# Another order of all steps of a gated MLP behind linear attention, and the low part of one w_sg tile through TensorE

## The chip, the cores and the metric

One core of a Trainium2 chip runs the whole kernel. The metric is the device time of one execution in microseconds, the median of the runs that are shown. Engines are named as the profile names them: PE is TensorE, PEld its weight loads, DVE is VectorE, ACT is ScalarE, POOL is GpSimd, SP is SyncE, which here only issues transfers.

## What is computed

Eight batches of eight heads, 576 positions of 64 channels. A linear attention first (softmax of q over its channels, softmax of k over positions), then a gated MLP on the heads' output x (576 x 512 for each batch):

```python
q_s = softmax of q over the channels          # exp(q - max) / (sum + 1e-9)
k_s = softmax of k over the positions
kv = np.einsum('bhsd,bhse->bhde', k_s, v)
x = np.einsum('bhsd,bhde->bhse', q_s, kv)     # heads side by side: 576 x 512

h = gelu(x @ w_in)                            # 512 x 1024, tanh form
u, v = h[..., :512], h[..., 512:]
v_n = (v - mean) / sqrt(var + 1e-6) * g_ln    # over the 512 channels
v_s = np.einsum('ts,bsd->btd', w_sg, v_n) + b_sg
out = x + (u * v_s) @ w_out                   # 512 x 512
```

w_in and w_out come as 64-bit numbers, the rest in 32 bits.

## The kernel before

All matmuls of the MLP run in three passes of a reduced 32-bit format: each operand is split into a high part (`_h`, the value rounded by a cast) and a low part (`_l`, the rest), and high x high, low x high and high x low are added in PSUM. So most steps come in such pairs: `x_high` and `x_low`, `wi_h` and `wi_l`, `gate_high` and `gate_low`.

The kernel is a list of some 1,220 named steps, `PLAN` (lines 28 to 129), each with its batch and tile numbers and, where there is a choice, the engine (A for ACT, V for DVE, G for POOL). The loop at line 657 calls them in that order. `InOrder` (line 136) ties every instruction of SP, DVE, ACT and POOL to the one before it on the same engine, and `mm` (line 231) does that for TensorE; so the list alone sets the order on every engine, and an instruction that waits holds back all behind it on its engine. Data and buffers are tracked by the tile framework, which puts in the waits between engines.

The steps, in the order in which a batch b goes through them:

- `load_q`, `load_k`, `load_v` (each for half h of the heads) and the loads of the weights are transfers that SP issues. Two halves have two buffers, so `load_k 1 0` overwrites what `kv_mm 0 0` reads.
- `wi_a` to `wi_d` take the bits of a 128-column tile f of w_in from 64 to 32 bits (ACT, then three times DVE); `wi_h` and `wi_l` split it. `wi_l` has three ways: POOL, DVE (V), or ACT (A) from PSUM after `wi_x`, in which TensorE adds identity x value and (minus identity) x high part. `wo_a` to `wo_l` do the same for w_out, `ws_h` and `ws_l` for tile i of w_sg (five tiles; the fifth is the tail of 64 rows).
- `k_ma`, `k_mb`, `k_mc`, `kt_mm`, `k_top`, `kb_mm`, `k_sub`, `k_exp`: maximum of k over positions (DVE, two transposes on TensorE between), subtraction and exp. `q_max`, `q_swapm`, `q_top`, `q_sub`, `q_exp`, `q_sum`, `q_swapd`, `q_inv`, `q_mul`, `q_turn`: softmax of q and its transposition.
- `kv_mm`, `kv_inv`, `kv_scale`, `x_mm`: the two products of the attention. `x_high` and `x_low` split x; `x_low` runs on DVE, or on ACT after `x_neg`, in which TensorE subtracts the high part in PSUM.
- `hu_mm` and `hv_mm`: x @ w_in for u (four tiles) and v (four tiles, and a fifth, the tail, for two batches at once). `hv_gelu`, `hv_sq`, `hv_stat`, `hv_pow`, `hv_norm`, `hv_high`, `hv_low`: activation and normalisation of v; `tail_high`, `tail_low`, `tail_again` for the tail.
- `sg_mm` multiplies with w_sg; its last two matmul pairs take the tail (`vn_1`, `vn_2`) and the bias. `gate`, `gate_high`, `gate_low`: product with u. `out_mm`, `out_add`, `out_rest`, `out_store`: product with w_out, x added, store.

PSUM has three double tiles (`ps2`: x, u, gate and output products, and in turn) and two single ones (`ps1`: the rest). So TensorE can start such a product when the one three (or two) before it in the same set was read out.

In the names of the trace below, `ps` is any PSUM tile, `ot_i` a tile of w_in under conversion, `vnh`, `vnl` and `vn` are the parts of v_n and of its tail, `km` and `qm` maxima, `raw_...` the buffers of 64-bit weights.

Of the kernel before, what the change touches and what calls it, by code (L numbers as in the profile page):

```python
# [28 lines left out]
load_q 0 1, q_max 0 1, q_swapm 0 1, q_top 0 1, q_sub 0 1 V, load_eye, load_w_in 0, load_w_in 1, load_q 0 0, load_b, load_w_in 3, load_k 0 1  # L29
load_w_in 2, load_k 0 0, load_w_in 5, wi_a 0, load_w_sg 2, load_v 0 0, load_w_sg 1, load_w_in 6, wi_a 1, neg, load_g, load_w_in 7, load_w_sg 0, wi_b 0  # L30
load_w_in 4, q_exp 0 1, wi_b 1, wi_c 0, load_v 0 1, load_w_out 0, wi_c 1, q_max 0 0, wi_a 3, q_swapm 0 0, wi_d 1, wi_d 0, wi_b 3, q_top 0 0, k_ma 0 1
wi_c 3, q_sum 0 1, q_sub 0 0, wi_h 1, wi_d 3, b_h, wi_h 0, wi_a 2, q_swapd 0 1, k_ma 0 0, wi_h 3, wi_x 1, wi_x 0, wi_b 2, k_mb 0 0, k_mb 0 1
q_exp 0 0, wi_l 0 A, wi_c 2, k_mc 0 1, k_mc 0 0, q_inv 0 1, wi_d 2, wi_l 1 A, kt_mm 0 0, k_top 0 0, wi_h 2, wi_x 3, q_sum 0 0, ws_h 2, q_mul 0 1 0
b_l, kb_mm 0 0, wi_l 3 A, k_sub 0 0, q_swapd 0 0, k_exp 0 0, kt_mm 0 1, k_top 0 1, kb_mm 0 1, q_inv 0 0, ws_l 2 V, wi_a 5, wi_a 7, kv_mm 0 0
k_sub 0 1, q_mul 0 0 0, load_k 1 0, q_mul 0 0 1, k_exp 0 1, wi_x 2, q_turn 0 0, kv_inv 0 0, q_mul 0 1 1, q_turn 0 1, kv_scale 0 0, wi_a 4, wi_l 2 A
ws_h 0, wi_b 7, x_mm 0 0, wi_b 4, wi_c 7, kv_mm 0 1, wi_c 4, x_high 0 0, x_high 0 1, wi_d 7, ws_l 0, wi_h 7, x_neg 0 1, x_neg 0 0, load_k 1 1
kv_inv 0 1, q_turn 0 3, q_turn 0 2, kv_scale 0 1, wi_a 6, x_low 0 0 A, wi_x 7, x_low 0 1 A, load_q 1 1, wi_d 4, load_w_out 1, load_w_out 3, x_mm 0 1
load_q 1 0, wi_h 4, wi_b 5, k_ma 1 0, wi_b 6, wi_x 4, x_high 0 2, x_high 0 3, k_mb 1 0, k_ma 1 1, x_neg 0 3, wi_l 7 A, k_mc 1 0, x_neg 0 2, wi_c 5
k_mb 1 1, ws_h 1, kt_mm 1 0, wi_c 6, k_mc 1 1, q_max 1 1, k_top 1 0, ws_l 1, wi_l 4 A, x_low 0 3 A, x_low 0 2 A, hu_mm 0 0, wo_a 0, q_swapm 1 1
kt_mm 1 1, kb_mm 1 0, wi_d 6, hu_mm 0 2, q_top 1 1, wi_d 5, k_top 1 1, q_max 1 0, wo_a 3, wi_h 6, wi_h 5, q_sub 1 1, k_sub 1 0, kb_mm 1 1, q_swapm 1 0  # L40
hu_mm 0 1, wi_l 6, q_exp 1 1, q_top 1 0, wo_b 3, k_sub 1 1, q_sub 1 0, k_exp 1 0, q_sum 1 1, k_exp 1 1, wi_l 5 V, wo_b 0, wo_c 3, q_swapd 1 1
load_v 1 0, load_v 1 1, kv_mm 1 0, hv_mm 0 0, load_v 2 0, load_k 2 0, load_w_out 2, load_w_sg 4, q_exp 1 0, q_inv 1 1, kv_inv 1 0, kv_scale 1 0
hu_gelu 0 1, q_mul 1 1 0, q_sum 1 0, hv_mm 0 3, q_mul 1 1 1, q_turn 1 2, q_swapd 1 0, wo_d 3, hv_gelu 0 0, q_inv 1 0, wo_c 0, hv_mm 0 2, hu_gelu 0 2
wo_a 1, q_mul 1 0 0 V, hv_gelu 0 3 A, hu_gelu 0 0, wo_b 1, q_turn 1 3, q_turn 1 0, q_mul 1 0 1, wo_a 2, kv_mm 1 1, q_turn 1 1, hv_gelu 0 2 A
# [131 lines left out]
def gmlp_kernel(ctx: ExitStack, tc: tile.TileContext, q, k, v, w_in, g_ln, w_sg, b_sg, w_out, identity, out):
# [529 lines left out]
```

## Time and profile before

| | |
|---|---|
| runs of the kernel before | 523.53, 519.97, 523.24 us |
| median | 523.24 us |
| profiled execution | 520.9 us, its span 519.1 us |
| granted clock of TensorE, mean | 0.99 |
| busy: PE, DVE, ACT, POOL | 489.8, 353.8, 258.7, 125.7 us |

The span runs from the first to the last instruction of the profiled execution; the time of an execution has a little around it. Idle time of an engine that is not the bound costs nothing. Durations of instructions that follow each other closely overlap by some hundredths of a microsecond.

### The profile page before, as it was taken

To read this page: it belongs to the slowest core of one execution; us is meant where nothing else is said; L and a number is where in the kernel's file an instruction comes from. 1 tells how busy PE (TensorE), PEld (TensorE's weight loads), DVE (VectorE), ACT (ScalarE), POOL (GpSimd) and SP (SyncE) were. 2 spreads that over 40 slices of the span, in tenths; PEclk is the share of its full clock that TensorE was granted. 3 is DMA by queue.
4 is the path that set the end of the run, shared out by engine and by line. 5 is a ranking of instruction groups with operands and counts; after the bars stand their busy time and mean duration, and the time that the engine had idled before them with its cause. 6 is when DMAs were issued, how large, how long until landed. Compare 5 with 4: busy or idle time off the path is not lost.

```text
span 519.1 us, 9328 instructions
## 1 busy us (share of the span) xinstructions
PE 489.8 (94%) x3852; PEld 447.0 (86%) x3852; DVE 353.8 (68%) x595; ACT 258.7 (50%) x506; POOL 125.7 (24%) x103
## 2 busy tenths in 40 slices
...
GB/s 284 377 208 270 218 169 1 2 97 115 131 162 129 98 3 137 1 52 47 223 50 70 61 232 19 29 1 189 108 1 0 47 47 1 1 0 69 2 23 92
DMA packets 19054, 48.87 MB, mean 94 GB/s; under 512 B 1602, under 2 KB 8132, under 8 KB 19012
## 3 DMA queue, kind: packets, MB, share of 16 engines
...
q14 instruction: 12, 0.10, 0.1%
...
## 4 chain that ended last, share of the span: by engine, by line
PE 81%; DVE 12%; DMA 4%; issue 1%; SPq 0%; ACT 0%; DVEq 0%
PE ps L232 81%; DVE ot_i L146 2%; DMA qq<-q 2%; DVE km L146 2%; DMA raw_vnh<-w_in 2%; DVE qm L146 1%; DVE ot_o L146 1%; DVE qd L146 1%; DMA kk<-k 1%; DVE qt L146 1%; DVE vnl L146 1%; DVE x_l L146 1%; DVE v L146 1%; SPq L146 0%; DVE o L146 0%
## 5 line engine op out<-in xcount | busy, mean ns | idle before, releaser
L146 POOL TENSOR_TENSOR rs<-ve,half 128x1 f32<-128x1 f32 x36 | 26.8, 753 | 141.4 <-DVE ve L146 141.4
L232 PE MATMUL ps<-ws_h,vnh 128*128 128x288 f32 x256 | 56.1, 300 | 0.0
L232 PE MATMUL ps<-gh,wo_h 128*128 128x288 f32 x256 | 56.0, 297 | 0.0
L232 PE MATMUL ps<-ulow,wo_h 128*128 128x288 f32 x256 | 55.5, 295 | 0.0
L232 PE MATMUL ps<-gh,wo_l 128*128 128x288 f32 x256 | 55.3, 295 | 0.0
L232 PE MATMUL ps<-ws_l,vnh 128*128 128x288 f32 x256 | 54.9, 295 | 0.0
L232 PE MATMUL ps<-ws_h,vnl 128*128 128x288 f32 x256 | 54.8, 295 | 0.0
L146 DVE TENSOR_TENSOR u<-ps,u 128x576 f32<-128x576 f32 x32 | 23.9, 752 | 43.2 <-PE ps L232 41.3
L146 ACT CAST gh<-u 128x576 fp32r<-128x576 f32 x32 | 21.1, 670 | 54.2 <-DVE u L146 54.1
L146 DVE TENSOR_TENSOR o<-ps,x_h 128x576 f32<-128x576 f32 (+1 forms) x33 | 23.6, 731 | 28.5 <-PE ps L232 28.5
L232 PEld LDWEIGHTS ps<-ws_h,vnh 128*128 128x128 f32 x256 | 41.4, 189 | 1.1 <-DVE u L146 0.4
L232 PEld LDWEIGHTS ps<-gh,wo_h 128*128 128x128 f32 x256 | 41.3, 188 | 0.6
L232 PEld LDWEIGHTS ps<-ws_h,vnl 128*128 128x128 f32 x256 | 41.3, 188 | 0.0
L232 PEld LDWEIGHTS ps<-gh,wo_l 128*128 128x128 f32 x256 | 41.3, 188 | 0.0
L232 PEld LDWEIGHTS ps<-ws_l,vnh 128*128 128x128 f32 x256 | 41.3, 188 | 0.0
L232 PEld LDWEIGHTS ps<-ulow,wo_h 128*128 128x128 f32 x256 | 41.3, 188 | 0.0
L146 ACT ACTIVATE v<-ps 128x512 f32<-128x512 f32 x36 | 21.4, 597 | 39.2 <-PE ps L232 37.5
L146 POOL TENSOR_TENSOR ulow<-u,gh 128x576 fp32r<-128x576 f32 x12 | 17.4, 1453 | 96.2 <-ACT gh L146 96.0
L232 PE MATMUL ps<-x_h,wi_h 128*128 128x288 f32 x256 | 40.5, 300 | 0.0
L232 PE MATMUL ps<-wi_h,x_h 128*128 128x512 f32 x144 | 40.1, 400 | 0.0
L232 PE MATMUL ps<-wi_l,x_h 128*128 128x512 f32 x144 | 39.5, 395 | 0.0
L232 PE MATMUL ps<-wi_h,x_l 128*128 128x512 f32 x144 | 39.3, 395 | 0.0
(105 smaller groups left out, 1068.1 us busy)
## 6 DMA issues: line engine op xcount, KB each, us to landing
...
```

The lines of the kernel that those rows point to most:

```text
L146: ins = op(*args, **kw)
L232: tc.keep_in_program_order(nc.tensor.matmul(*args, **kw))
```

## The change

The table of steps is replaced as a whole by another order of nearly the same steps. What differs in kind:

- w_sg tile 0 gets its low part from ACT out of PSUM, after a new step `ws_x 0` of TensorE (as `wi_x` does for w_in); before, POOL made it.
- `x_neg` with `x_low` on ACT is kept for pairs 0 and 1 of batch 0 only; before, also for pairs 2 and 3 of batch 0 and pair 1 of batch 1. These `x_low` now run on DVE.
- `wi_x` is there for tiles 0, 3, 5 and 6 of w_in; before, for 0, 1, 2, 3, 4 and 7. Tiles 2 and 7 get their low part on DVE (before: 5), tiles 1 and 4 on POOL (before: 6).
- ws_l 1 goes from POOL to DVE, ws_l 4 from DVE to POOL. Many of `hv_gelu`/`hv_stat`, `gate_low`, `out_rest`, `q_mul` and `q_sub` change engine, in both directions.
- `b_l` may be given an engine (it is not), and functions for another way to the sum of q, with an input for it, are new but no step of the list calls them (`load_blk`, `qs_mm`, `q_rec`, `qr_mm`, `q_by`).

```diff
 PLAN = """
-load_q 0 1, q_max 0 1, q_swapm 0 1, q_top 0 1, q_sub 0 1 V, load_eye, load_w_in 0, load_w_in 1, load_q 0 0, load_b, load_w_in 3, load_k 0 1
+load_w_in 1, load_w_in 3, load_w_in 0, load_w_in 2, load_q 0 0, load_eye, load_k 0 0, load_q 0 1, load_w_in 6, wi_a 1, load_w_sg 2, load_w_sg 1
...
-    kr_s = slots("kr", 2, [P, 2])
+    kr_s, qr_s = slots("kr", 2, [P, 2]), slots("qr", 2, [QC, 4 * NQ])
+    blk = sb("blk", [P, 2])
...
+    def ws_x(i):
+
+        ps = bank(ps2, "sx", i)
+        for j in range(2):
+            cs = slice(j * (WT // 2), (j + 1) * (WT // 2))
+            mm(ps[:, j, 0:WT // 2], eye, raw_sg(i)[:, cs], start=True, stop=False)
+            mm(ps[:, j, 0:WT // 2], minus, (ws_h[:, i] if i < ST else ws_1)[:, cs], start=False, stop=True)
+
     def ws_l_(i, E=G):
         hi, lo = (ws_h[:, i], ws_l[:, i]) if i < ST else (ws_1[0:TL], ws_2[0:TL])
+        if E is A:
+            A.copy(out=lo.rearrange("p (j n) -> p j n", j=2), in_=st["sx", i][0:lo.shape[0], :, 0:WT // 2])
+            return
         E.tensor_tensor(out=lo, in0=raw_sg(i)[0:lo.shape[0]], in1=f32(hi), op=ALU.subtract)
...
+    arr["blocks"] = np.ascontiguousarray(np.repeat(np.eye(2, dtype=np.float32), D, axis=0))
```

The first place is SP's queue, some 20 transfers into the program. In the names, `kk0_0` and `kk1_0` are k of batches 0 and 1, half 0 (one buffer), `vv0_1` is v of batch 0, half 1, `ghws_...` a raw tile of w_sg, `raw_wo_...` raw tiles of w_in at this point, `raw_x_h` one of w_out. Before:

```order
L146 DMA ghws_0_132<-w_sg 128x640
L146 DMA raw_wo_h_88<-w_in 128x4x256
L146 DMA vv0_1_139<-v 128x1300
L146 DMA raw_x_h_89<-w_out 128x4x256
L146 DMA kk1_0_251<-k 128x1280
L146 DMA kk1_1_313<-k 128x1280
```

And in the changed kernel:

```order
L148 DMA raw_wo_h_88<-w_in 128x4x256
L148 DMA kk1_0_250<-k 128x1280
L148 DMA ghws_4_261<-w_sg 128x640
L148 DMA vv0_1_264<-v 128x1300
L148 DMA raw_x_h_90<-w_out 128x4x256
L148 DMA g_bc_67<-g_ln 128x512
```

The load of k for batch 1 stood behind both loads of v of batch 0, and now stands ahead of the second, with the fifth tile of w_sg between them.

The second place is DVE just ahead of the first `sg_mm`. `vnl` is the low part of v_n (`hv_low`), `vn_10` the tail (`tail_low 0`), the last thing that the first `sg_mm` needs; `qm2_0` and `qm2_1` are the row maxima of q of batch 2 (`q_top`), `km2_1` maxima of k. Before:

```order
L146 SCALAR_TENSOR_TENSOR vnl_788<-v0_1_747,rs0_1_811,vnh_787 128x512
L146 TENSOR_TENSOR km2_1_829<-km2_1_829 128x256
L146 SCALAR_TENSOR_TENSOR vnl_788<-v0_2_634,rs0_2_847,vnh_787 128x512
L146 TENSOR_TENSOR qm2_0_844<-qm2_0_844,qs2_0_871 128x36
L146 TENSOR_TENSOR km2_1_829<-km2_1_829,kk2_1_672 128x256
L146 SCALAR_TENSOR_TENSOR vn_10_71<-v0_4_832,rs0_4_880,vn_10_71 64x512
```

And in the changed kernel:

```order
L148 SCALAR_TENSOR_TENSOR v0_2_744<-v0_2_744,nm0_2_776,g_bc_67 128x512
L148 SCALAR_TENSOR_TENSOR vnl_756<-v0_0_638,rs0_0_742,vnh_755 128x512
L148 TENSOR_TENSOR qq2_0_641<-qq2_0_641,qm2_0_709 128x1152
L148 SCALAR_TENSOR_TENSOR vnl_756<-v0_2_744,rs0_2_819,vnh_755 128x512
L148 SCALAR_TENSOR_TENSOR vn_10_71<-v0_4_801,rs0_4_844,vn_10_71 64x512
L148 TENSOR_TENSOR km2_1_814<-km2_1_814,kk2_1_654 128x256
L148 TENSOR_REDUCE qm2_1_905<-qq2_1_688 128x36
```

The maxima of q of batch 2, half 1, and the last one of k have moved behind the tail.

The third place is POOL at the same point of the program, from the last `hv_pow` of batch 0 (`rs0_4`) on; `qq2_1<-qq2_1,qm2_1` is `q_sub 2 1`, `wo_l` the low part of w_out. Before:

```order
L146 TENSOR_TENSOR rs0_4_880<-ve0_4_865,half_70 128x1
L146 TENSOR_TENSOR rs1_2_928<-ve1_2_877,half_70 128x1
L146 TENSOR_TENSOR qq2_1_654<-qq2_1_654,qm2_1_809 128x1152
L146 TENSOR_TENSOR wo_l_695<-ot_o_2_610,wo_h_694 128x4x128
L146 TENSOR_TENSOR wo_l_695<-ot_o_0_403,wo_h_694 128x4x128
```

And in the changed kernel:

```order
L148 TENSOR_TENSOR rs0_4_844<-ve0_4_841,half_70 128x1
L148 TENSOR_TENSOR wo_l_600<-ot_o_1_452,wo_h_599 128x4x128
L148 TENSOR_TENSOR qq2_1_688<-qq2_1_688,qm2_1_905 128x1152
L148 TENSOR_TENSOR rs1_3_1006<-ve1_3_965,half_70 128x1
L148 TENSOR_TENSOR qq2_0_641<-qq2_0_641,qd2_0_953 128x576
L148 TENSOR_TENSOR wo_l_600<-ot_o_2_529,wo_h_599 128x4x128
```

One low part of w_out has moved ahead of `q_sub 2 1`, the other two behind it; and `q_sub 2 1` needs `qm2_1`, which DVE now makes behind the tail.

## Rows read from the trace of the kernel before

**Rows 1.** The page: span, and busy time of each engine.

```profile
span 519.1 us, 9328 instructions
PE 489.8 (94%) x3852; PEld 447.0 (86%) x3852; DVE 353.8 (68%) x595; ACT 258.7 (50%) x506; POOL 125.7 (24%) x103
```

**Rows 2.** The chain that ended last, in order of time: start, length, what.

```profile
135.73 378.25 PE ps L232 x2970
```

**Rows 3.** Timeline of TensorE: start, length, instructions, in brackets idle time before.

```profile
28.02 2.44 PE L232 MATMUL ps<-vv,kk 128*64 128x65 f32 x40 [0.28 <-ACT kk L146]
...
32.95 1.39 PE L232 MATMUL ps<-vv,kk 128*64 128x65 f32 x40
...
38.65 1.12 PE L232 MATMUL ps<-ot_i,eye 128*128 128x512 f32 x2
...
39.99 0.80 PE L232 MATMUL ps<-x_h,minus 128*128 128x288 f32 x4
...
40.92 1.31 PE L232 MATMUL ps<-x_h,wi_h 128*128 128x288 f32 x8
...
83.57 0.43 PE L232 MATMUL ps<-ws_h,vnh 128*128 128x288 f32 x2
...
86.50 0.42 PE L232 MATMUL ps<-ws_l,vnh 128*128 128x288 f32 x2
89.94 0.80 PE L232 MATMUL ps<-ws,vn 128*128 128x288 f32 x4 [3.02 <-DVE vn L146]
...
106.42 0.54 PE L232 MATMUL ps<-gh,wo_h 128*128 128x288 f32 x2
...
135.73 0.44 PE L232 MATMUL ps<-eye,km 128*128 128x128 f32 x2 [0.43 <-DVE km L146]
```

**Rows 4.** Windows: stretch, length, busy PE, PEld, DVE, ACT, POOL, clock, DMA, GB/s.

```profile
0.00:90.00 90.00, 66.22 (x487) 50.30 (x487) 82.25 (x144) 67.24 (x145) 37.17 (x29) 0.94 0.63 220
20.00:30.00 10.00, 6.57 (x47) 4.17 (x49) 9.18 (x17) 7.06 (x14) 5.41 (x5) 0.52 0.99 342
40.92:83.57 42.65, 42.53 (x317) 35.77 (x316) 41.36 (x77) 35.23 (x85) 19.31 (x14) 1.00 0.50 184
136.00:514.00 378.00, 377.97 (x2970) 353.11 (x2968) 226.19 (x378) 166.36 (x316) 76.33 (x65) 1.00 0.19 63
```

**Rows 5.** Timeline of DVE just ahead of the first sg_mm's wait.

```profile
82.82 0.19 DVE L146 TENSOR_TENSOR qm<-qm,qs 128x36 f32<-128x36 f32 x1
...
83.65 0.42 DVE L146 TENSOR_TENSOR km<-km 128x256 f32<-128x256 f32 x1
...
84.64 2.13 DVE L146 TENSOR_TENSOR qm<-qm,qs 128x36 f32<-128x36 f32 x1
86.69 1.53 DVE L146 TENSOR_TENSOR km<-km,kk 128x256 f32<-128x256 f32 x1
88.26 1.63 DVE L146 SCALAR_TENSOR_TENSOR vn<-v,rs,vn 64x512 fp32r<-64x512 f32 x1
```

**Rows 6.** Timeline of POOL in the same stretch.

```profile
84.11 2.61 POOL L146 TENSOR_TENSOR qq<-qq,qm 128x1152 f32<-128x1152 f32 x1
86.68 2.67 POOL L146 TENSOR_TENSOR wo_l<-ot_o,wo_h 128x512 fp32r<-128x512 f32 x2
```

**Rows 7.** Groups of DVE instructions: busy us, mean ns of one, idle before.

```profile
L146 DVE TENSOR_REDUCE qm<-qq 128x36 f32<-128x1152 f32 x16 | 21.5, 1348 | 16.5 <-DMA qq<-q 16.3
L146 DVE TENSOR_TENSOR x_l<-ps,x_h 128x576 fp32r<-128x576 f32 x27 | 19.9, 748 | 5.3 <-ACT x_h L146 5.2
...
L146 DVE TENSOR_TENSOR qq<-qq,qd 128x576 f32<-128x576 f32 x14 | 11.2, 819 | 0.0
...
L146 DVE SCALAR_TENSOR_TENSOR vn<-v,rs,vn 64x512 fp32r<-64x512 f32 x8 | 6.9, 858 | 3.3 <-ACT vn L146 3.2
```

**Rows 8.** Start of DVE; then, of the k tile from 25 to 60 us, issue to landing.

```profile
5.69 1.35 DVE L146 TENSOR_REDUCE qm<-qq 128x36 f32<-128x1152 f32 x1 [2.24 <-DMA qq<-q]
...
DMA to landing us min/median/max: 4.0/4.7/5.5
```

More of the change, by code (lines that the diff above doesn't have):

```diff
@@ L24 @@
 WT = S + TL
+NQ = 6
+QC = S // NQ
 PLAN = """
[L29 to L32 removed]
@@ L33 @@
[L33 to L44, printed above, removed]
@@ L61 @@
-x_high 2 0, q_swapd 3 0, load_v 3 1, hv_high 1 0, x_low 2 0, k_mc 3 0, hv_low 1 0, k_ma 3 1, kt_mm 3 0, kv_scale 2 1, hu_mm 1 0, q_inv 3 0, k_top 3 0
-q_swapm 3 1, x_high 2 1, q_top 3 1, x_low 2 1, k_mb 3 1, hu_gelu 1 2, hu_gelu 1 0, k_mc 3 1, q_sub 3 1 V, kt_mm 3 1, kb_mm 3 0, sg_mm 1 0, k_top 3 1
-q_exp 3 1, q_mul 3 0 1 V, k_sub 3 0, kb_mm 3 1, sg_mm 1 1, q_mul 3 0 0 V, q_sum 3 1, sg_mm 1 2, q_turn 3 1, k_sub 3 1, k_exp 3 1, gate 1 1, q_turn 3 0
-q_swapd 3 1, gate 1 0, load_q 4 0, k_exp 3 0, gate_high 1 1, gate_high 1 0, x_mm 2 1, gate 1 2, q_inv 3 1, kv_mm 3 0, x_high 2 3, gate_low 1 0
```

205 lines of the change are left out of this document (122 added, 83 removed).

## The prediction

> **What bounds the kernel now.** I read the page first: TensorE is busy for 489.8 of 519.1 us, VectorE (DVE) for 353.8 [rows 1]. That alone says that TensorE is the bound, but it is an average, so the next view is the chain that ended last: its last long piece is TensorE alone, 378.25 us and 2970 matmuls without a break, from 135.73 us on [rows 2]. The time by windows says the same of 136 to 514 us: 377.97 of 378 us busy, while DVE has 226.19 [rows 4]. No reordering can gain there; it can only lose. What is left to gain is ahead of 136 us. In the first 90 us TensorE is busy for 66.22 and DVE for 82.25 [rows 4]: DVE is the bound of the head. The timeline of TensorE shows what that costs: the first hu_mm 0 0 starts at 40.92, work is then dense up to 86.9, in the middle of the first sg_mm (started at 83.57), and there TensorE waits 3.02 us for DVE (tail_low 0, tile vn). One more wait of 0.43 us follows at 135.73 [rows 3].
>
> I therefore cut the time into three: up to the first hu_mm 0 0, from there to the first sg_mm, and from there to the end.
>
> **From the first sg_mm to the end.** Before: 519.1 - 83.57 = 435.5 us, of which 3.0 + 0.4 us are the two waits; 432.1 without them. The changed plan has the same steps of TensorE behind its first sg_mm, with kt_mm 2 0 moved in (two transposes, under 0.4 us), and the same five DVE additions and the same stores behind the last matmul. So 432.3 us, if TensorE never waits. Where a wait could come is the first out_mm 0: DVE has, by the mean durations of its steps, some 18 us of work between tail_low 0 and gate_low 0 3 (an estimate over 27 steps), and TensorE 16.5 us up to out_mm (89.94 to 106.42 [rows 3]), with some 2.4 us of slack, since out_mm takes the four gated tiles one after another; I cost it at nothing here and give the lack of that cover to a rival.
>
> **From hu_mm 0 0 to the first sg_mm.** 42.65 us before, 42.53 of it busy [rows 4]. The same steps after, less x_neg 1 1 (0.4 us: four such matmuls, two steps, took 0.80 [rows 3]) and two small pairs of transposes: 42.0 us.
>
> **Up to hu_mm 0 0.** Removed from TensorE: two of six wi_x (38.65 to 39.99, 1.34 us each) and two of four x_neg of batch 0 (0.4 us each); added: ws_x 0. No row shows ws_x; it is the same two kinds of matmul over 640 columns instead of 512, so 0 us (where TensorE sits idle anyway) to 640/512 x 1.34 = 1.7 us, twice that at the lower clock. It stands where TensorE waits for DVE, so I take nothing for it, nor for the removed ones as such. Functions and an input that the plan never calls cost nothing: they issue no instruction.
> What counts is when the data comes. DVE starts at 5.69 us when the first transfer (q) lands, and 576 KB of it [rows 8]; the first is now w_in 1, 512 KB, and one step of ScalarE on it, for which I allow 0.7 us: about 6.2 us. Ahead of k_sub 0 0 DVE then has about 5 us less to do than before (q_sub 0 1, both q_sum, q_inv 0 1 and the k maxima of half 1 come later, wi_l 2 comes in). But ScalarE now has ws_h 0, ws_h 2 and a swap ahead of k_exp 0 0, so that kv_mm 0 0, at 28.02 before, starts at about 25.2 and, at the 2.44 us that it took at half clock [rows 3], ends at 27.6. Here the order of SP's queue matters: load_k 1 0 overwrites kk 0 0 and so waits for kv_mm 0 0, and load_w_sg 4 and load_v 0 1 now stand behind it; before, both v loads stood ahead. A k load takes 4.7 us to land (4.0 to 5.5 [rows 8]): 32.4; the 970 KB behind it at 342 GB/s [rows 4] take 2.9 us more: v 0 1 is there at 35.2, with 4.0 or 5.5 in place of 4.7 at 34.5 or 36.0. Before, kv_mm 0 1 started at 32.95 and hu_mm 0 0 followed 7.97 us later [rows 3]; without x_neg 0 2 and 0 3 (0.8 us) 7.2 us. That gives 42.4 us, in bounds of 41.7 and 43.2. I take 42.3, so 1.4 us later than before, and the first sg_mm at 42.3 + 42.0 = 84.3.
>
> **Is DVE there in time?** The first sg_mm needs tail_low 0 3.35 us after its start: at 87.65. Before, DVE was through with it at 89.9, with 82.25 us of work and 7.65 idle [rows 4]. Two things change. First the list ahead of tail_low 0: out go q_max 2 1 (1.35), k_top 2 0, q_top 2 1 and k_mc 2 1 (together about 1.0), in come x_low 0 2, 0 3 and 1 1 (0.75 each), wi_l 7 and q_mul 0 0 1 (0.7 to 0.8 each): net +1.5 us [rows 7]. Second, the last three instructions before that wait took 2.13, 1.53 and 1.63 us, where the like of the first took 0.19 and of the second 0.42 just before, and the third takes 0.86 in the mean of its eight and 0.75 without this one [rows 5, 7]: together 3.9 us too long. Each ends when a POOL instruction ends: q_sub 2 1 ran from 84.11 for 2.61, then two wo_l from 86.68 for 2.67 [rows 6]. In the changed order q_sub 2 1 cannot start there, since q_top 2 1 and so its wait come behind tail_low 0, and wo_l 2 and wo_l 0 stand behind it on POOL; only wo_l 1 is left. So 82.25 + 1.5 - 3.9 = 79.9 of work, and, with the same idle time, DVE is through at 87.5. Bounds: 91.4 with none of the 3.9 gone, and as far below 87.5, 83.6, if as much again goes earlier in the head.
> The Trainium skill, SBUF — State Buffer, Who interferes with whom, states the rule behind these rows: a VectorE instruction with two inputs in SBUF and a GpSimd instruction that reads SBUF exclude each other, and the second waits out the first. The trace agrees in the three cases. By that rule the change also brings new chances of it, since it puts ws_l 1, wi_l 2, wi_l 7 and q_mul 0 0 1 on DVE, all with two SBUF inputs; by rows, it costs what rival 3 says.
>
> **The sum.** 84.3 + 432.3 = 516.6 us of span, against 519.1: -2.5. The profiled execution took 520.9, 1.8 more than its span, so 518.4 for the like of it. The median of the runs is 523.24, 2.3 over that execution; on it the same difference gives **520.7 us**.
>
> **Rivals.** (1) Ending slower: the SP queue. v 0 1 and w_sg 4 hang on kv_mm 0 0. ScalarE waits in order on ws_h 4 with b_h and x_high 0 0 behind it, TensorE on kv_mm 0 1. Each microsecond by which kv_mm 0 0 ends after 27.6 moves hu_mm 0 0, and the end, by one. Past 30.1 the gain is gone; at 33 the time is 526. For it speaks that every step ahead of kv_mm 0 0 is a chain of three engines; against it, that DVE has 5 us less ahead of it.
> (2) The clock. Between 20 and 30 us the granted clock was 0.52 on average, 1.2 for most of it instead of 2.4 GHz, in a stretch in which TensorE was busy for 6.57 of 10 us [rows 4]. After, TensorE has fewer steps before hu_mm 0 0 and new idle time while v 0 1 is on its way, so the lower level may last to 40 us: kv_mm 0 1 at 2.44 for 1.39 [rows 3], x_mm 0 1 and wi_x 5 about 1.2 more each: +3.5, so 524.2. The Trainium skill, TensorE: Matmul & The Clock Gate, Part 1, says that the lower level is the default and activity lifts it, which by itself gives the same 524.2.
> (3) DVE stays late: other pairs of DVE and POOL instructions collide as often (bound 91.4 above). The first sg_mm then waits 3.7 us as before: 524.4.
> (4) More than forecast: kv_mm 0 0 by 25, k and v landing at the short end, hu_mm 0 0 at 40, DVE ready at 84: -5 or better, 518 or less.
> (5) Nothing: what the head gains is lost in the first out_mm 0, where DVE's 18 us get 2 to 3 longer by collisions: 523.
>
> **Chances.** Forecast (518.5 to 522.5) 0.45; rival 1 0.14, rival 2 0.10, rival 3 0.10, rival 4 0.14, rival 5 0.07. About 1% is what a measurement of this kernel can tell from no change, since its own three runs lie 0.7% apart: faster by more is under 518.0, most of rival 4 and an edge of the forecast: 0.17. Slower by more is over 528.5, the far end of rivals 1 and 2, or an unseen wait in the dense part: 0.13. Within 1%: 0.70. The range from 515.5 to 526.5 holds the forecast, rivals 2, 3 and 5 and the near parts of 1 and 4.
>
> **What the changed profile would show.** hu_mm 0 0 at 42.3; the first sg_mm at 84.3 with no wait for vn in its last part over 0.5 us; no POOL instruction of 2 us beside tail_low 0; from the first out_mm 0 to the end TensorE without a wait over 0.5 us. Wrong would be a start of hu_mm 0 0 past 45 (rivals 1, 2: the clock row tells which), a wait for vn (rival 3), or waits behind 136 us, for which I saw no reason.

## The result, and the profile after

| | before | after |
|---|---|---|
| median (13 runs each) | 521.51 us (518.27 to 523.56) | 516.99 us (516.37 to 518.03) |
| ratio | | 0.9914, 95% interval 0.9898 to 0.9930 |
| profiled execution, its span | 520.9, 519.1 us | 518.03, 515.9 us |
| first `hu_mm 0 0` starts | 40.92 | 43.36 |
| first `sg_mm` starts | 83.57 | 84.37 |
| first `sg_mm` to the end | 435.5 us | 431.5 us |

The change saves 0.9%: within the 1% that I called about no change, but clearly measured. In the two profiled executions the span is 3.2 us shorter. The medians moved by 4.5 us; where the rest of that comes from is a part of the experiments.

The page and the windows of after, to be read beside [rows 1, 4] (columns of the windows as there):

```profile
span 515.9 us, 9312 instructions
PE 488.9 (95%) x3846; PEld 446.2 (86%) x3846; DVE 352.9 (68%) x597; ACT 251.1 (49%) x491; POOL 136.2 (26%) x110
```

```profile
20.00:30.00 10.00, 6.53 (x50) 4.03 (x50) 9.90 (x20) 9.01 (x18) 4.67 (x5) 0.66 0.72 243
30.00:40.00 10.00, 7.12 (x61) 4.60 (x62) 9.69 (x18) 5.83 (x10) 4.00 (x4) 0.51 1.00 330
136.00:511.00 375.00, 374.69 (x2957) 349.88 (x2955) 224.72 (x381) 160.94 (x307) 88.76 (x71) 1.00 0.18 65
```

TensorE is still the bound: 374.69 of 375 us busy behind 136 us. The clock column shows the price in the head: the clock is now low (1.2 GHz, half) mostly between 30 and 40 us, where it was low between 20 and 30 before.

The timeline of TensorE (start, length, instructions, in brackets the idle time before), to be read beside [rows 3]:

```profile
31.64 2.20 PE L235 MATMUL ps<-qt,kvt 64*64 64x288 f32 x16 [4.11 <-DVE kvt L148]
35.08 2.43 PE L235 MATMUL ps<-vv,kk 128*64 128x65 f32 x40 [1.24 <-ACT x_h L148]
...
43.36 1.23 PE L235 MATMUL ps<-x_h,wi_h 128*128 128x288 f32 x8
...
84.37 0.43 PE L235 MATMUL ps<-ws_h,vnh 128*128 128x288 f32 x2
...
87.54 0.69 PE L235 MATMUL ps<-ws,vn 128*128 128x288 f32 x4
...
106.33 0.54 PE L235 MATMUL ps<-ulow,wo_h 128*128 128x288 f32 x2 [0.16 <-POOL ulow L148]
...
108.19 0.53 PE L235 MATMUL ps<-ulow,wo_h 128*128 128x288 f32 x2 [0.79 <-DVE ulow L148]
```

The row at 87.54 is the one that had 3.02 us of waiting ahead of it; now it has none. In its place there is a new, smaller stall in the first out_mm (the rows at 106.33 and 108.19): that step lasts from 104.15 to 108.99, 4.84 us, where the later ones take 3.35. The chain of waits (start, length, what) names the same pair of instructions as its last pieces ahead of the dense part:

```profile
104.84 1.45 POOL ulow L148
106.31 1.83 DVE ulow L148
108.19 134.45 PE ps L235 x1116
...
257.04 253.77 PE ps L235 x1978
```

Timeline of DVE ahead of `tail_low 0` (tile vn), and of POOL around it, to be read beside [rows 5, 6]:

```profile
81.92 1.79 DVE L148 SCALAR_TENSOR_TENSOR vnl<-v,rs,vnh 128x512 fp32r<-128x512 f32 x1
...
84.91 0.74 DVE L148 SCALAR_TENSOR_TENSOR vnl<-v,rs,vnh 128x512 fp32r<-128x512 f32 x1
85.68 0.74 DVE L148 SCALAR_TENSOR_TENSOR vn<-v,rs,vn 64x512 fp32r<-64x512 f32 x1
```

```profile
81.72 1.44 POOL L148 TENSOR_TENSOR wo_l<-ot_o,wo_h 128x512 fp32r<-128x512 f32 x1
91.76 2.13 POOL L148 TENSOR_TENSOR qq<-qq,qm 128x1152 f32<-128x1152 f32 x1 [8.60 <-issue]
...
97.16 1.74 POOL L148 TENSOR_TENSOR wo_l<-ot_o,wo_h 128x512 fp32r<-128x512 f32 x1
```

POOL is idle for the 8.6 us around `tail_low 0`, which takes 0.74 us instead of 1.63 and ends at 86.42 (forecast 87.5); TensorE comes to it at 87.54. Only one instruction of DVE is still stretched there: 1.79 instead of 0.74 us, beside `wo_l 1`.

### The profile page after: what moved, and what is told of

It reads as the page before. It is cut to its first block, busy times and chain, and to the rows that moved or that the text cites. A ratio compares the mean times of both kernels' runs of the same rounds, so it can differ in the third digit from the quotient of the medians.

```text
span 515.9 us, 9312 instructions
## 1 busy us (share of the span) xinstructions
PE 488.9 (95%) x3846; PEld 446.2 (86%) x3846; DVE 352.9 (68%) x597; ACT 251.1 (49%) x491; POOL 136.2 (26%) x110
## 4 chain that ended last, share of the span: by engine, by line
PE 86%; DVE 9%; DMA 3%; ACT 1%; issue 1%; POOL 0%; SPq 0%
PE ps L235 86%; DMA qq<-q 2%; DVE ot_i L148 1%; DMA raw_vnh<-w_in 1%; DVE qd L148 1%; DVE kk L148 1%; DVE qm L148 1%; DVE qt L148 1%; DVE ulow L148 1%; DVE u L148 1%; DVE km L148 1%; DVE qq L148 0%; DVE o L148 0%; DVE v L148 0%; POOL ulow L148 0%
## 5 line engine op out<-in xcount | busy, mean ns | idle before, releaser
L148 POOL TENSOR_TENSOR rs<-ve,half 128x1 f32<-128x1 f32 x36 | 28.4, 788 | 113.0 <-DVE ve L148 111.7
L148 DVE TENSOR_TENSOR u<-ps,u 128x576 f32<-128x576 f32 x32 | 24.0, 754 | 46.5 <-PE ps L235 41.7
L148 POOL TENSOR_TENSOR qq<-qq,qm 128x1152 f32<-128x1152 f32 x12 | 26.1, 2176 | 78.5 <-DVE qm L148 54.4
L148 POOL TENSOR_TENSOR ulow<-u,gh 128x576 fp32r<-128x576 f32 x16 | 22.9, 1433 | 87.8 <-ACT gh L148 73.3
L235 PEld LDWEIGHTS ps<-gh,wo_h 128*128 128x128 f32 x256 | 41.7, 188 | 1.0
```

What stands on the lines that cost most here:

```text
L148: ins = op(*args, **kw)
L235: tc.keep_in_program_order(nc.tensor.matmul(*args, **kw))
```

## The experiments

Theory: TensorE waited 3 us because POOL's `q_sub 2 1`, `wo_l 2` and `wo_l 0` ran beside DVE's last three instructions ahead of `tail_low 0`, and the change moved them away. Rivals: DVE was late by its amount of work; or the gain comes from another part of the change. Starts and ends of steps below are read from each kernel's own timeline. Medians of different experiments stand on different chips; ratios are to runs of before on the same one.

**One step moved in the kernel before.**

```diff
 (kernel before, PLAN)
-..., hv_high 0 2, q_swapm 2 0, q_top 2 1, hv_stat 1 2 A
+..., hv_high 0 2, q_swapm 2 0, hv_stat 1 2 A
-..., k_mc 2 1, tail_low 0, sg_mm 0 2, q_sub 2 0 V
+..., k_mc 2 1, tail_low 0, q_top 2 1, sg_mm 0 2, q_sub 2 0 V
```

> The kernel before with one step moved: q_top 2 1 behind tail_low 0, so that the swap-free part of POOL's list, q_sub 2 1 with wo_l 2 and wo_l 0 behind it, cannot start before VectorE is through with tail_low 0. Theory (the collisions are the wait): q_top 2 0, k_mc 2 1 and tail_low 0 take about 0.2, 0.4 and 0.75 us instead of 2.13, 1.53 and 1.63, tail_low 0 ends near 86.0 instead of 89.9, the first sg_mm has no wait for vn over 0.3 us, and the span goes from 519.1 to about 516.3 (2.5 to 3.0 less). Rival A (VectorE is late by its sheer amount of work, and other pairs collide): tail_low 0 still ends past 89, wait over 2 us, span within 0.7 of before. Rival B (the wait only moves): the wait for vn goes, but waits for gate_low or k_sub of 2 us and more turn up between 90 and 112 us, and the span is within 1 us of before. The spread of before (5.3 us over 13 runs): if the collisions make it, the runs of this kernel lie within 2.5 us; if the clock's lower stretch in the head makes it, they lie as wide as those of before.

Measured: 516.75 against 522.26 us, ratio 0.9902 (0.9883 to 0.9922): all of what the whole change gives. The timelines of DVE, POOL and TensorE:

```profile
83.99 0.18 DVE L146 TENSOR_TENSOR qm<-qm,qs 128x36 f32<-128x36 f32 x1
84.10 0.42 DVE L146 TENSOR_TENSOR km<-km,kk 128x256 f32<-128x256 f32 x1
84.55 0.75 DVE L146 SCALAR_TENSOR_TENSOR vn<-v,rs,vn 64x512 fp32r<-64x512 f32 x1
```

```profile
85.65 3.13 POOL L146 TENSOR_TENSOR qq<-qq,qm 128x1152 f32<-128x1152 f32 x1 [2.17 <-issue]
```

```profile
86.22 0.70 PE L232 MATMUL ps<-ws,vn 128*128 128x288 f32 x4
```

The last three instructions of [rows 5] now take 0.18, 0.42 and 0.75 us instead of 2.13, 1.53 and 1.63, since POOL starts behind them; `tail_low 0` ends at 85.29, and TensorE does not wait. Both rivals fall: the amount of DVE's work is the same, and the only later wait of TensorE is one of 0.53 us (0.43 before). From the first sg_mm to the end it takes 432.3 us (before 435.5); the other 0.6 us of the span's 3.8 lie in the head, where an unchanged list also differs between executions (below). The Trainium skill, SBUF — State Buffer, Who interferes with whom, states the exclusion that the prediction cited for this; the three durations agree. What the expectation hoped to read from the spread it can't: the 6 runs lie within 2.8 us, and the 11 of before on that chip lie within 2.6.

**POOL's work put back beside `tail_low 0`.**

```diff
 (changed kernel, PLAN)
+..., hv_pow 0 3, wo_h 3, wo_h 1, wo_h 0, ...
+hv_pow 0 4, wo_l 1, wo_l 2, wo_l 0, hv_sq 1 1, ...
 (and these four taken out of their places further down)
```

> The changed kernel with wo_l 2 and wo_l 0 put back right behind wo_l 1 on POOL (and wo_h 0 on ScalarE behind wo_h 1 for it), so that POOL has 4 us of subtractions of two SBUF inputs from about 81.7 us on, beside hv_low 0 0, q_sub 2 0, hv_low 0 2 and tail_low 0. Theory (collisions of POOL and VectorE make the wait): VectorE's instructions there become 1 to 3 us longer in all, tail_low 0 ends at 87.5 to 89.5 instead of 86.4, and the first sg_mm (84.4) waits 0.3 to 1.9 us for vn; in return gate_low 0 3 no longer runs beside wo_l 0 and takes 0.75 instead of 1.83 us, which gives about 1 us back in the first out_mm 0. Net: span within 1 us of the changed kernel's 515.9. Rival (the wait of before was VectorE's amount of work): tail_low 0 ends within 0.5 us of 86.4, no wait for vn, and the span is 1 us under the changed kernel's.

Measured: 517.50 us, ratio 0.9910 (0.9893 to 0.9926); span 515.3. The timelines of POOL, DVE and TensorE:

```profile
80.96 5.48 POOL L148 TENSOR_TENSOR wo_l<-ot_o,wo_h 128x512 fp32r<-128x512 f32 x3
```

```profile
82.87 2.45 DVE L148 TENSOR_TENSOR qq<-qq,qm 128x1152 f32<-128x1152 f32 x1
85.24 1.75 DVE L148 SCALAR_TENSOR_TENSOR vnl<-v,rs,vnh 128x512 fp32r<-128x512 f32 x1
87.03 0.74 DVE L148 SCALAR_TENSOR_TENSOR vn<-v,rs,vn 64x512 fp32r<-64x512 f32 x1
```

```profile
87.05 0.53 PE L235 MATMUL ps<-ws_h,vnl 128*128 128x288 f32 x2 [1.42 <-DVE vnl L148]
```

The wait is back as soon as POOL's work is: two instructions are 1.1 and 1.0 us too long, and TensorE waits 1.42 us for the second, which is not `tail_low 0` but the `hv_low` ahead of it. The span is not longer, since the first out_mm, without `wo_l 0` beside `gate_low 0 3`, takes 3.35 us instead of 4.84. So a collision has a price only where its DVE instruction is waited for.

**One part alone: x_low on DVE, without x_neg.**

```diff
 (kernel before, PLAN)
-..., x_neg 0 3, ..., x_neg 0 2, ..., x_low 0 3 A, x_low 0 2 A, ..., x_neg 1 1, x_mm 1 1, x_low 1 1 A
+..., x_low 0 3, x_low 0 2, ..., x_mm 1 1, x_low 1 1
```

> The kernel before with one part of the change alone: x_low 0 2, 0 3 and 1 1 on VectorE (TENSOR_TENSOR out of the bank) instead of x_neg on TensorE and a copy on ScalarE. TensorE has six matmuls (1.2 us) less ahead of the first sg_mm, VectorE 2.2 us more. Theory (VectorE is the bound of the head): the first sg_mm starts up to 1.2 us earlier, tail_low 0 ends about 2 us later than in the kernel before, the wait for vn grows from 3.0 to about 5 to 6 us, and the span is 1 to 2.3 us more. Rival (TensorE sets the head, the wait is a matter of which instructions collide): the wait for vn stays at 3.0 or below and the span is 0.5 to 1.2 us less.

Measured: 525.04 against 520.94 us, ratio 1.0071 (1.0042 to 1.0100): slower, and the rival falls. The expected place was wrong, though. A row of TensorE's timeline, and one of its waits (us in total, times, longest):

```profile
44.58 0.80 PE L232 MATMUL ps<-x_l,wi_h 128*128 128x288 f32 x4 [1.66 <-DVE x_l L146]
```

```profile
PE ps L232 <- DVE vn L146: 3.1, 1, 3.1
```

The wait for vn did not grow; `hu_mm 0 0` itself waits 1.66 us for x_l, and everything behind moves with it: the first sg_mm starts at 83.69, where an unchanged list had 81.95 in the second profile of before (below) and 83.57 in the first. TensorE's saved 1.2 us is paid back by the engine that sets the head. The median is 4.1 us longer; no run shows where all of that lies.

**One part undone: ws_x 0.**

```diff
 (changed kernel, PLAN)
-..., q_swapd 0 0, ws_x 0, k_mb 0 1, ...
+..., q_swapd 0 0, k_mb 0 1, ...
-load_k 1 0, ws_l 0 A, q_inv 0 1, ...
+load_k 1 0, ws_l 0, q_inv 0 1, ...
```

> The changed kernel with one part undone: ws_x 0 (four matmuls of TensorE) is gone and ws_l 0 is a subtraction on POOL again, not a copy by ScalarE. Theory (the part was worth nothing, it only used idle time): ws_x 0 ran from 19.9 to 24.1 us, where TensorE waited for VectorE's k maxima anyway; kv_mm 0 0 starts at 24.5 to 25.1 as before, hu_mm 0 0 within 0.8 us of the changed kernel's 43.4, the time within 1 us of it. Rival A (POOL's 1.4 us on ws_l 0 fall on VectorE's subtractions in the head): VectorE comes 1 us and more later to kv_scale 0 0, and hu_mm 0 0 with it. Rival B (without ws_x 0 TensorE is idle for 4 us more and the clock is lower for longer): kv_mm 0 0 takes 2.4 us, x_mm 0 0, kv_mm 0 1 and wi_x 6 run at 0.5, hu_mm 0 0 starts past 44.

Measured: 518.49 against 521.04 us, ratio 0.9947 (0.9922 to 0.9972); span 516.5. The timelines of DVE and POOL:

```profile
22.69 2.03 DVE L148 SCALAR_TENSOR_TENSOR ot_i<-raw_wo_l,ot_i 128x512 uint32<-128x512 uint32 x1
```

```profile
22.54 1.64 POOL L148 TENSOR_TENSOR ws_l<-ghws,ws_h 128x640 fp32r<-128x640 f32 x1 [0.66 <-ACT ws_h L148]
```

Rival A: the subtraction falls on `wi_c 6`, which takes 2.03 instead of 0.68 us; the k maxima behind it on DVE are 1.7 us later, and so is `kv_mm 0 0` (26.67 instead of 25.01). `hu_mm 0 0` starts at 44.01, 0.65 us later than in the changed kernel's profile and 1.4 and 2.0 later than in two others with the same list up to there (next experiment). So the part is worth something in the head, not nothing, and by the same mechanism; the spread of the head leaves open how much. Whether the 1.5 us between this median and the changed kernel's is all of it stays open, since the two stand on different chips.

**What sets the start of `hu_mm 0 0`: clock or queue?** Two changes to the changed kernel.

```diff
 (changed kernel, PLAN; warm n: n matmuls minus x wi_h, 128x512, into a free bank)
-..., kb_mm 0 1, wi_h 6
+..., kb_mm 0 1, warm 9, wi_h 6
```

> The changed kernel with nine extra matmuls (minus times wi_h of tile 0, 128x512) into a free bank behind kb_mm 0 1, in the 4.1 us in which TensorE waits for kvt; their result is overwritten by x_mm 0 0. Theory (the idle time brings the clock down, rival 2 of the prediction): the granted clock stays at 1.0 for most of 30 to 40 us instead of 0.5; kv_mm 0 1 takes 1.4 instead of 2.43, wi_x 6 about 1.3 instead of 2.3, and hu_mm 0 0 starts at 41.0 to 41.8 instead of 43.4, since from there kv_scale 0 1 of VectorE (ending at 39.1) sets x_mm 0 1; span 1.5 to 2.3 less, about 514. Rival A (the stretch of the lower clock is not caused by this idle time): clock and hu_mm 0 0 as in the changed kernel, span within 0.5 us. Rival B (VectorE sets the head): the clock is up, but hu_mm 0 0 starts no earlier than 43.0.

```diff
 (changed kernel, PLAN)
+..., load_w_in 5, load_v 0 1, ...
-load_k 1 0, ..., load_w_sg 4, q_mul 0 0 0, load_v 0 1, ...
+load_w_sg 4, load_k 1 0, ..., q_mul 0 0 0, ...
```

> The changed kernel with two transfers moved in the queue of SP: load_v 0 1 up behind load_w_in 5, and load_w_sg 4 ahead of load_k 1 0, so that neither stands behind the transfer that waits for kv_mm 0 0. Theory (rival 1 of the prediction: the queue sets kv_mm 0 1): v 0 1 lands near 27 instead of 34.9, kv_mm 0 1 starts right behind x_mm 0 0, at about 33.9 instead of 35.1, and hu_mm 0 0 1.0 to 1.3 us earlier, at about 42.2; span 1.0 to 1.3 less. Rival A (VectorE sets this stretch: kv_inv 0 1 and kv_scale 0 1 stand behind its other work until 39.1): kv_mm 0 1 starts earlier, but x_mm 0 1 no earlier than 40.3 and hu_mm 0 0 less than 0.5 us earlier. Rival B (576 KB more ahead of kv_mm 0 0 delay the transfers that feed it): kv_mm 0 0 starts later than 25.5 and the gain is gone.

Measured: 516.78 us, ratio 0.9898 (0.9881 to 0.9915), and 516.72 us, ratio 0.9899 (0.9881 to 0.9917): neither can be told from the changed kernel. `hu_mm 0 0` starts at 42.85 and 42.55, at 43.36 in the changed kernel's profile. With the extra matmuls, the window and TensorE's timeline read:

```profile
30.00:40.00 10.00, 5.40 (x69) 3.40 (x67) 9.97 (x18) 6.97 (x11) 4.55 (x4) 1.00 1.01 356
```

```profile
34.95 1.39 PE L235 MATMUL ps<-vv,kk 128*64 128x65 f32 x40 [1.57 <-DMA vv<-v]
...
39.99 0.44 PE L235 MATMUL ps<-eye,km 128*128 128x128 f32 x2 [1.84 <-DVE kvt L148]
```

The clock is at 1.00 (2.4 GHz) instead of 0.51, and `kv_mm 0 1` takes 1.39 us instead of 2.43, as forecast; but TensorE then waits 1.57 us for v 0 1 and 1.84 us for DVE. So with matmuls in the idle time the clock stays up, and little is gained, because DVE (9.97 of 10 us busy) is the bound there. How little, these starts can't tell: two kernels of this section leave the list up to `hu_mm 0 0` as it is, the one with POOL's work put back (first row) and the one with `gate_low 0 3` moved (the other two), and in them it starts at 42.62 and 42.00:

```profile
42.62 1.23 PE L235 MATMUL ps<-x_h,wi_h 128*128 128x288 f32 x8
```

```profile
39.14 0.44 PE L235 MATMUL ps<-eye,km 128*128 128x128 f32 x2 [0.91 <-DVE kvt L148]
...
42.00 1.23 PE L235 MATMUL ps<-x_h,wi_h 128*128 128x288 f32 x8
```

In both, at a clock of 0.66 and 0.67 between 30 and 40 us, TensorE waits for DVE's `kv_scale 0 1` (0.53 and 0.91 us), so the low clock costs nothing there. In the changed kernel's own profile it does not wait for it, since v 0 1 landed later and TensorE at half clock was the later of the two. The low clock and the late v together therefore cost from nothing to 1.4 us (43.36 - 42.00), not the 3.5 of rival 2. Moving the transfers takes away the wait for v alone; its 0.8 us, between its theory and its rival A, lie within the same spread, and DVE is waited for in that kernel too, 1.19 us at the same place. That second kernel's span (516.5) was longer all the same, by two waits far behind, 0.65 us at 256.76 and 0.64 at 276.33. The first (timelines of ScalarE and of TensorE):

```profile
254.57 0.92 ACT L148 COPY qs<-qm 32x36 f32<-32x36 f32 x4 [11.55 <-DVE qm L148]
255.51 1.19 ACT L148 ACTIVATE u<-ps 128x576 f32<-128x576 f32 x2
```

```profile
256.76 0.53 PE L235 MATMUL ps<-ws_h,vnh 128*128 128x288 f32 x2 [0.65 <-ACT u L148]
```

`q_swapm 6 0` holds ScalarE until a q transfer (issued at 243.42, landed 9.74 us later, behind k and v ones) and `q_max 6 0` are done; two `hu_gelu` stand behind it, and `sg_mm 3 0` waits for them. In the changed kernel's profile the same chain runs to 257.04 and just fails to stall TensorE.

**The stall in the first out_mm.**

```diff
 (changed kernel, PLAN)
-gate_low 0 1 / gate_high 0 2, kv_inv 2 0, q_turn 2 1, kv_scale 2 0, wo_h 0, gate_low 0 2 G, load_q 3 0, gate_low 0 3, ...
+gate_low 0 1, gate_low 0 3 / gate_high 0 2, kv_inv 2 0, q_turn 2 1, kv_scale 2 0, wo_h 0, gate_low 0 2 G, load_q 3 0, ...
```

> The changed kernel with gate_low 0 3 moved up on VectorE, ahead of kv_inv 2 0, so that it runs before POOL's gate_low 0 2 and not beside POOL's wo_l 0. Theory (the first out_mm waits for the two gate_low only because POOL and VectorE exclude each other there): gate_low 0 3 takes 0.75 us instead of 1.83, the first out_mm lasts 3.4 to 3.8 us instead of 4.84, and the span is 1.0 to 1.4 less than the changed kernel's with the same start of the first sg_mm. Rival (POOL's gate_low 0 2 is itself late): the first out_mm still lasts over 4.4 us and the span gains less than 0.4.

Measured: 518.10 against 520.94 us, ratio 0.9945 (0.9918 to 0.9973), no faster than the changed kernel (0.9914); the first out_mm still lasts 4.81 us. The rival, and my reading of the wait, were both short of the cause. The timelines of POOL and DVE:

```profile
103.46 1.42 POOL L148 TENSOR_TENSOR ulow<-u,gh 128x576 fp32r<-128x576 f32 x1 [5.95 <-ACT gh L148]
```

```profile
104.92 1.82 DVE L148 TENSOR_TENSOR ulow<-u,gh 128x576 fp32r<-128x576 f32 x1 [1.60 <-POOL ulow L148]
```

DVE had nothing to do for 1.60 us and did not start `gate_low 0 3` before POOL's `gate_low 0 2` ended. The five buffers of `u_s` explain it: `gate_low 0 3` writes the one that holds u 0 2, which `gate_low 0 2` reads. It is a data dependence first, and the collision with `wo_l 0` (1.82 instead of 0.75 us) comes on top. An estimate for the changed kernel: from its start at 106.31, `gate_low 0 3` would have been done in 0.75 us at 107.06, and TensorE ran out of work at 107.40 (108.19 less 0.79); so the 0.79 us are the collision's, to which the dependence led, and the 0.16 us ahead are the late `gate_low 0 2`. In a later kernel (below), with `gate_low 0 2` on DVE, the two take 1.55 us together and the first out_mm 3.35.

**Why the medians moved more than the profiles.** First the kernel before once more:

> The kernel before once more, unchanged, for a second profile. Its 24 runs so far lie between 518.3 and 523.6 us and their mean granted clock (0.986 to 0.997) does not go with the time. Theory (the wait for tail_low 0 differs between executions, since whether POOL and VectorE instructions of 0.7 to 2.6 us fall on each other hangs on a few tenths of a us): in a profile whose span is over 520 the wait for vn in the first sg_mm is 4 us or more, or there is another wait of 1 us and more behind a stretched VectorE instruction in the first 120 us, and behind 136 us nothing differs by more than 0.5 us. Rival A (the start of the head differs: transfers or clock): hu_mm 0 0 starts at 41.9 or later and the wait for vn is 3.0 us or less. Rival B (the dense part differs): the stretch from 136 us to the end differs by 1 us and more.

Measured: 522.02 us in its own runs, span of the profile 520.1. TensorE's timeline, and the windows around the wait:

```profile
88.33 1.33 PE L232 MATMUL ps<-ws,vn 128*128 128x288 f32 x4 [3.02 <-DVE vn L146]
```

```profile
80.00:87.00 7.00, 5.30 (x34) 4.66 (x32) 6.90 (x12) 6.78 (x16) 6.30 (x5) 1.00 0.00 0
87.50:94.30 6.80, 5.97 (x25) 5.96 (x26) 6.67 (x11) 3.59 (x4) 0.23 (x1) 0.50 0.00 1
94.30:120.00 25.70, 25.70 (x216) 24.82 (x215) 21.57 (x32) 12.65 (x25) 6.96 (x5) 1.00 0.15 50
```

No expectation held. The wait is the same 3.02 us; the head is earlier (`hu_mm 0 0` at 38.82, not 40.92; `kv_mm 0 0` takes 2.44 us in both, so TensorE ran alike there, and where the 2.1 us come from stays open); but behind the wait the clock falls to half for 6.8 us, which the first profile did not show. `sg_mm 0 0` takes 6.02 us instead of 3.98, and the stretch from the first sg_mm to the last out_mm of batch 0 takes 38.75 us against 36.07: 2.7 us. The kernel with x_low on DVE shows it too (0.76 in the same window). So the wait cost 3.0 us in one execution of before and 5.7 in another. Then the same kernel with TensorE kept busy in the wait:

```diff
 (kernel before, sg_mm(0, 2), ahead of its last two pairs)
+for _ in range(12):
+    mm(columns4(spare[:, 0]), minus, parts("i", 0)[0], start=True, stop=True)
```

> The kernel before with twelve extra matmuls (minus times wi_h of tile 0, 128x512, into the bank that the next sg_mm overwrites) put into its first sg_mm, right ahead of the two vn pairs, so that TensorE works through the 3 us in which it waited for tail_low 0. In a second profile of before the granted clock fell to 0.5 from 87.49 to 94.31, behind that wait, and sg_mm 0 0 took 6.0 us instead of 4.0; in the first profile it stayed at 1.0. Theory (the wait costs 3.0 us and in many executions 2 to 3.4 us more by the clock): the profile shows 1.0 from 80 to 120 us, the wait for vn is under 0.5 us behind the extra matmuls, the first sg_mm ends where it did (about 3 us late), and the median is 1 to 2.5 us under that of before, with nothing else changed. Rival (the lower stretch does not come from the wait, or is rare): the median is within 0.5 us of before, or up to 0.5 above.

The window behind the wait, in this kernel:

```profile
87.50:94.30 6.80, 6.45 (x47) 6.03 (x47) 6.70 (x11) 3.75 (x4) 0.26 (x2) 1.00 0.00 1
```

Measured: 520.68 against 521.04 us, ratio 0.9987 (0.9961 to 1.0014). The clock stays at 1.00, and the same stretch takes 36.17 us, as in the first profile, where it stayed up without them; the 12 runs lie within 3.4 us where 23 of before on that chip lie within 7.4. But the median moved by 0.4 us, which is no difference, so this does not show that the clock makes the rest of the 4.5 us. What is sure: 1.6 us of it is which executions were profiled (before's 0.6 under its median, after's 1.0 over), and an execution of before can be 2.7 us longer behind a wait that after no longer has. How many are stays open, and so does what else makes before's runs differ: the head's 2.1 us between two profiles of one list are as large.

**Towards a faster kernel.** Three kernels, each from the one ahead of it: first all the moves that the profiles asked for; then `gate_low 0 2` on DVE and eight extra matmuls; then `hu_mm 0 0` ahead of `kb_mm 1 0`.

```diff
 (the first, from the changed kernel, PLAN; each of these steps taken out where it stood)
+..., load_w_in 5, load_v 0 1, ...
+load_w_sg 4, load_k 1 0, ...
+..., kv_scale 0 0, k_sub 0 1, k_exp 0 1, ...
+..., k_mb 1 0, kv_inv 0 1, kv_scale 0 1, ..., wi_b 7, k_mc 1 0, wi_c 5, wi_d 5, wi_c 7, ...
+wo_l 2, wo_l 1, ..., gate_low 0 1, gate_low 0 3
+..., hu_gelu 3 1, hu_gelu 3 0, q_max 6 0, ..., gate_low 3 3, q_max 6 1, ...
```

> The changed kernel with what its own profile asks for, as moves of steps alone: load_v 0 1 and load_w_sg 4 ahead of load_k 1 0 on SP; k_sub 0 1 and k_exp 0 1 behind kv_scale 0 0; kv_inv 0 1, kv_scale 0 1, k_mc 1 0 and wi_d 5 ahead of wi_c 5 and wi_c 7 on VectorE; wo_l 1 behind wo_l 2 on POOL; gate_low 0 3 ahead of kv_inv 2 0; hu_gelu 3 1 and 3 0 ahead of q_swapm 6 0 on ScalarE, which waits for a q transfer, and gate_low 3 3 ahead of q_max 6 1 on VectorE, which waits for one too. Theory: x_mm 0 0 starts near 30.5 instead of 31.6, hu_mm 0 0 at 40.3 to 41.5 instead of 43.4, the first sg_mm at 81.3 to 82.5 with a wait for vn under 0.5 us (hv_low 0 0 no longer runs beside wo_l 1, so that VectorE is through with tail_low 0 by 84.5), the first out_mm lasts 3.4 to 3.8 us, and no wait of TensorE over 0.3 us follows: span 512 to 513.5, some 2.5 to 4 us under the changed kernel's. Rival (VectorE's work is the bound of the head whatever the order): hu_mm 0 0 starts earlier but the wait for vn takes 1.5 us and more of it, span 514 to 515.

```diff
 (the second, from the first)
+..., kb_mm 0 1, warm 8, ...
+..., x_mm 0 1, kt_mm 1 0, ...
-..., gate_low 0 1, gate_low 0 3 / gate_high 0 2, ..., wo_h 0, gate_low 0 2 G, ...
+..., gate_low 0 1, gate_high 0 2, tail_again 1, gate_low 0 2, gate_low 0 3, wo_l 3 V / kv_inv 2 0, q_turn 2 1, kv_scale 2 0, wo_h 0, q_turn 2 0, ...
```

> The rearranged kernel (the one with all moves) with three more edits. In that one gate_low 0 3 still started only when POOL's gate_low 0 2 had ended, since it writes the buffer of u 0 2 that gate_low 0 2 reads: so gate_low 0 2 goes to VectorE, with gate_high 0 2 ahead of it and tail_again 1 ahead of wo_h 0 (so that wo_l 0 starts on POOL behind gate_low 0 3), and wo_l 3 and q_turn 2 0 behind both; eight extra matmuls behind kb_mm 0 1 keep TensorE busy where it waits for kvt; kt_mm 1 0 goes behind x_mm 0 1. Theory: the first out_mm lasts 3.4 to 3.7 us instead of 4.81, hu_mm 0 0 starts 0.5 to 1.5 us earlier than its 42.07, VectorE's 2.2 us of slack at tail_low 0 covers that, and the span is 512.0 to 513.3 instead of 514.8. Rival A (VectorE's other work is late instead, since gate_low 0 2 adds 0.75 us to it): k_sub 2 1, kv_mm 2 1 or the next gates make TensorE wait, span over 514. Rival B (the clock in the head does not answer to eight matmuls): hu_mm 0 0 at 41.8 to 42.3, span 513.3 to 514.

```diff
 (the third, from the second)
+..., wi_l 6 A, x_low 0 1 A, x_mm 0 1, x_high 0 3, x_high 0 2, kt_mm 1 0, wi_h 5, k_top 1 0, wi_c 7, x_low 0 2, x_low 0 3, wi_d 7, load_w_out 2, hu_mm 0 0
+kb_mm 1 0, q_max 1 0, wi_x 5, ...
+..., gate 0 3, kv_inv 2 0, kv_scale 2 0, ...
```

> The kernel of the last experiment (all moves, extra matmuls, gate_low 0 2 on VectorE), with what made TensorE wait in it put right. There kb_mm 1 0 waited 1.9 us for k_top 1 0, hu_mm 0 0 started at 44.2 behind it, with the clock at 0.5 for 3.4 us, and kb_mm 2 1 waited 0.7 us for kv_scale 2 0. Now hu_mm 0 0 goes ahead of kb_mm 1 0 and wi_x 5; x_low 0 1, x_high 0 3 and x_high 0 2 ahead of wi_h 5 on ScalarE; k_top 1 0, x_low 0 2 and x_low 0 3 ahead of wi_c 7, wi_d 7 and q_max 1 0 on VectorE; kv_inv 2 0 and kv_scale 2 0 right behind gate 0 3. Theory: hu_mm 0 0 starts at 40.3 to 41.2 (with 1.5 us of TensorE's work, kb_mm 1 0 and wi_x 5, now behind it), the first sg_mm at 82.5 to 83.3 with a wait for vn of 0.3 us at most, the first out_mm lasts 3.4 us, 430.1 us from the first sg_mm to the end: span 512.6 to 513.5, median of the runs 1.0 to 2.0 us under the 516.2 of the last one. Rival (VectorE is the bound of the head: what TensorE gains at hu_mm 0 0 is waited for again): the first sg_mm waits 1 us and more for vn, or hu_mm 0 0 does so for x_l, and the span is over 514.

Measured: 516.73 us (ratio 0.9911, 0.9879 to 0.9944), 516.22 us (0.9896, 0.9860 to 0.9933) and 517.16 us (0.9928, 0.9904 to 0.9951). None can be told from the changed kernel, nor from the one with a single step moved. All three missed their forecasts, which began at 512 to 512.6 us of span and ended at 513.3 to 513.5: the profiles have 514.8, 516.4 and 517.1, the last two taken of the slowest execution of their kernel (518.26 and 519.05 us). What each gained at one place it lost at the next; in the second, by the timelines of TensorE and DVE:

```profile
41.59 0.66 PE L235 MATMUL ps<-eye,kt 128*128 128x128 f32 x2 [1.92 <-DVE kt L148]
```

```profile
104.91 1.55 DVE L148 TENSOR_TENSOR ulow<-u,gh 128x576 fp32r<-128x576 f32 x2 [0.36 <-ACT gh L148]
```

The first out_mm is dense (3.35 us), but `kb_mm 1 0` now waits for `k_top 1 0`, and `hu_mm 0 0` starts at 44.18 in this profile. In the third it starts at 41.44, yet `kt_mm 3 0` waits 1.59 us for DVE's `k_mc 3 0` (TensorE's timeline):

```profile
120.18 0.41 PE L235 MATMUL ps<-eye,km 128*128 128x128 f32 x2 [1.59 <-DVE km L148]
```

## Why the prediction was right, and where not

1. **Bound, and where there was something to gain: right.** TensorE is dense behind 136 us in both, and the wait that the change takes away lies ahead of it.
2. **Up to `hu_mm 0 0`: 42.3 forecast, 43.36 measured, outside its bounds (41.7 to 43.2).** Two other executions of the same list had 42.62 and 42.00, inside them. The queue was read rightly: `kv_mm 0 0` ends at 27.16 (27.6 forecast), v 0 1 lands at 34.94 (35.2). The miss is the clock: I let `kv_mm 0 1` and what follows run at full speed, and they ran at half, as rival 2 said; but its price, the late v included, was at most 1.4 us, not 3.5, because DVE's `kv_scale 0 1` is ready only at 39.1 us or later and sets the start where TensorE is earlier. With the clock held up, DVE takes that place (42.85).
3. **To the first sg_mm: 42.0 forecast, 41.0 measured.** By luck it makes up for point 2, so that 84.37 stands beside the forecast 84.3. Besides x_neg and the transposes, the same 32 matmuls of x_mm take 0.6 us less there and hu_mm 0.3 less; no run shows why.
4. **`tail_low 0` in time: right, and this is the change.** Forecast 87.5, measured 86.42: 80.4 us of work and 6.0 idle, where I had 79.9 and 7.6. Moving `q_top 2 1` alone shows the cause that the prediction named. One reading was loose: the third of the three instructions ended at 89.89, not with POOL's last one (89.35) but 0.5 us behind it. DVE's list being 1.5 us longer did no harm, though the x_low part of it by itself makes the kernel before slower.
5. **From there to the end: 432.3 forecast, 431.5 measured.** It holds a stall of 1.5 us that I had costed at nothing (rival 5's place): the 2.4 us of slack of the first out_mm assumed that the four `gate_low` are independent and undisturbed, and they are neither. Without it the rest takes 430.0 us: from the start of each matmul to that of the next, waits left out, hu_mm, sg_mm and x_mm of the same count take 0.6, 1.0 and 0.5 us less than in before. This goes with the list and not with the execution: the kernel before with one step moved takes 432.3 us over this stretch, 0.5 of it a wait. No run shows why; the matmuls stand in another order there.
6. **ws_x 0 at nothing: mis-sized.** Taking it out makes `kv_mm 0 0` 1.7 us later and `hu_mm 0 0` 0.65 to 2.0.
7. **The level: the term that was furthest off.** I put the profile's difference on the median, as if every execution paid what the profiled one did. The difference of the spans was forecast as 2.5 us and is 3.2; that of the medians is 4.5, and the time of 516.99 us is 3.7 under my 520.7. 1.7 us of that is only that before's median over 13 runs is 521.51 and not the 523.24 of the three runs I had; the other 2.0 us are the effect. The range (515.5 to 526.5) held it, but it was 11 us wide. The time lies under the forecast (518.5 to 522.5), where rival 4 had it (518 or less), and not by rival 4's way: `kv_mm 0 0` did start at 25, but `hu_mm 0 0` at 43.36 and not 40, and DVE was ready at 86.42 and not 84.
